# A down stage with a lag of six chunks, and weight statistics and residual loads moved, in a fused linear-attention and feed-forward kernel

## Chip, core and metric

The kernel runs on one core of one Trainium2 chip. The metric is the device time of one execution in microseconds (us). The engines are called by the profile's names: PE (TensorE matmul) and PEld (its weight load), DVE (VectorE), ACT (ScalarE), POOL (GpSimd) and SP (the queue that issues most DMAs). Each of them works through its own instructions in order.

## What is computed

All inputs are bf16. There are 2048 tokens, D = 1024, 32 heads of 32, F = 3584.

```python
xn = layernorm(x)
q, k, v = split(xn @ wqkv)                       # phi(t) = where(t > 0, t + 1, exp(t)) + 1e-6
kv = einsum("bhsd,bhse->bhde", phi(k), v);  z = sum_s phi(k)
s  = (phi(q) @ kv / (phi(q) . z + 1e-6)) @ wo
g  = silu((silu(xn @ w_gate) * (xn @ w_up)) @ w_down)
out = x + s * g
```

## The kernel before

The work has four stages on PE. **KV** (to about 132 us): layer norm, K and V projections and the sum kv over 16 token tiles. **Q and attention** (to 256 us): four blocks of 512 tokens; the Q product of block b+1 runs beside the division (`emit_ND`, L613) of block b, a DMA transpose on SP turns its result (`emit_OT`, L642), and `emit_S` (L647) multiplies by wo. The result s goes to a scratch tensor `s_dram` in DRAM. **Gate and up** (GU) and **down**, both twice: each pass takes 1024 tokens, the upper half first (256 to 430 and 517 to 686 us for GU, 430 to 517 and 686 to 772 us for down).

GU and down use a Strassen-Winograd scheme: every 2x2 block product is made of seven products and not eight. It needs sums of blocks of the activations (S1 to S4) and of the weights (T1 to T4), kept in fp16. The T of the weights are made on chip once, on POOL (`emit_T`, L267, four tensor-tensor operations), and the tile with its T is written to DRAM for the second pass (L286, L287, L290). So that fp16 does not overflow, each weight tile is scaled by a power of two first. That is the **statistics**: a Square with accumulation on ACT (`emit_st0`, L248), a one-column matmul that adds up the partitions (`emit_st1`, L252), and on DVE three small operations and the scaling of the tile (`emit_st2`, L257 to L265).

A weight tile is named by a key: 14 column groups of w_gate ("g") and of w_up ("u"), 14 row groups of w_down ("w"). `prep_q` (L295) lists the keys that are prepared already in the KV and attention stages: 12 of g, 9 of w, and the first g and u last. `prep(n)` makes n steps of this pipeline; a step loads one tile, starts the Square of the previous one and finishes the one before that. Steps are placed by hand: ten in KV (L558), three in the Q product of block 0 (L583), two in the attention of block 0, which stands beside the Q product of block 1, and four in each later block (L674). The other tiles ("raw") are prepared inside GU of the first pass: `pipe`, `pipe1`, `pipe2` for gate and up, `wd_pipe`, `wd_pipe1`, `wd_pipe2` for w_down, one w tile in four iterations.

GU runs over 28 keys, i = 0 to 27. An iteration issues `emit_a(i+1)` (four products of four 128x512 matmuls, banks y, x and the double bank zw), then `emit_b(i)` (three products into x and zw of key i), then `emit_evac(i)`, which on DVE and ACT forms the hidden activations h. Of the zw banks there are two, so the zw products of `emit_a(i+2)` wait for the DVE operation L787 of key i. When all statistics are known, `emit_lam` (L802, eight small DVE operations) derives a factor for each of the 14 row groups, and `scale_h` (L817) multiplies h by it, on ACT or DVE. `emit_hs` (L827) then makes S1 to S4 of a pair of chunks of h for one half of the tokens, four operations on DVE (on POOL for the first pair).

The down stage (`emit_down`, L875) takes 256 tokens at a time as a pair of token tiles t0, t1. A chunk is one of the 14 row groups of w_down. Phase a has four matmuls a chunk (`step_a`), phase b three (`step_b`). The tile t1 follows t0 by `LEAD` = 4 chunks:

```python
NS = NFG + LEAD
for st in range(NS):
    ...
    if st < NFG:
        step_a(t0, st)
        if st == NFG - 1:
            evac_a(t0, hf == 0)
    if st >= LEAD:
        step_a(t1, st - LEAD)
```

PSUM has four single banks (x, y) and two double banks (zw), so with t0 and t1 in flight it is full, and each new tile waits until DVE has emptied the bank of the tile two before. `more_S` and `next_S` are calls of `emit_hs` (with `scale_h` in the first pass) written between the steps. The final pair of the last pass (`finish`, L967) runs t1 eight chunks behind t0 (`LEADZ`), interleaved up to the end of t0, and then the last eight chunks product by product. `fin` (L865) multiplies by s, adds x and writes out; its three engine arguments say who multiplies, adds and issues the store. In `finish` some of these go to POOL (`G`). The residual pieces of x and s that `fin` needs are loaded by `io_load` (L854); five are loaded ahead, at the start of the first GU, and each `fin` loads one more.

DVE, ACT, PE and POOL follow the order of the program; SP too in the attention stage, while in GU and down the order on SP is chosen by the framework's scheduler.

Of the kernel before, what the change touches and what calls it, by code (L numbers as in the profile page):

```python
# [21 lines left out]
def kernel(  # L22
# [39 lines left out]
    NPREP = 12  # L62
    NWE = 9
    LEAD = 4
    LEADZ = 8
# [8 lines left out]
    persist = ctx.enter_context(tc.tile_pool(name="persist", bufs=1))  # L74
    dram = ctx.enter_context(tc.tile_pool(name="dram", bufs=1, space=DRAM))
    xnp = ctx.enter_context(tc.tile_pool(name="xnp", bufs=NB))
    wgu = ctx.enter_context(tc.tile_pool(name="wgu", bufs=NPK))
    stp = ctx.enter_context(tc.tile_pool(name="stp", bufs=4))
    p12 = ExitStack()
    psA = p12.enter_context(tc.tile_pool(name="psA", bufs=3, space=PSUM))  # L80
    ps1 = ExitStack()
    psB = ps1.enter_context(tc.tile_pool(name="psB", bufs=3, space=PSUM))
    psC = ps1.enter_context(tc.tile_pool(name="psC", bufs=2, space=PSUM))
# [33 lines left out]
    w12 = p12.enter_context(tc.tile_pool(name="w12", bufs=1))  # L117
    wo_sb = w12.tile([P, G, D], BF16, name="wo_sb")
    wq_sb = w12.tile([P, DC, D], BF16, name="wq_sb")
    late = p12.enter_context(tc.tile_pool(name="late", bufs=1))  # L120
# [38 lines left out]
    blk12 = blk12_es.enter_context(tc.tile_pool(name="blk12", bufs=2, side="right"))  # L159
    phiw = p12.enter_context(tc.tile_pool(name="phiw", bufs=2))  # L160
# [94 lines left out]
    def emit_st2(key, t, act=False):  # L255
        tot = stp.tile([P, 1], I32, name="tot", tag="tot")
        nc.vector.tensor_scalar(out=tot[:], in0=st_tiles.pop(key).bitcast(I32), scalar1=1, scalar2=0x3f800000,  # L257
                                op0=ALU.logical_shift_right, op1=ALU.bitwise_and)
        c = kcol(key)
        ri, ci = rc_all[:, c:c + 1].bitcast(I32), cs_all[:, c:c + 1].bitcast(I32)  # L260
        nc.vector.tensor_scalar(out=ri, in0=tot[:], scalar1=52 << 23, scalar2=None, op0=ALU.add)
        nc.vector.tensor_scalar(out=ci, in0=ri, scalar1=-1, scalar2=254 << 23, op0=ALU.mult, op1=ALU.add)
        w = raw_view(key, t)
        if not act:
            nc.vector.tensor_scalar(out=w, in0=w, scalar1=cs_all[:, c:c + 1], scalar2=None, op0=ALU.mult)  # L265
# [29 lines left out]
    prep_q = deque(gkeys[2:2 + 2 * NPREP:2] + wkeys[0:NWE] + gkeys[0:2])  # L295
# [33 lines left out]
    with ExitStack() as p1:  # L329
        wpool = p1.enter_context(tc.tile_pool(name="p1w", bufs=1))  # L330
        work = p1.enter_context(tc.tile_pool(name="p1work", bufs=2))
        xnw = p1.enter_context(tc.tile_pool(name="p1xn", bufs=4))
        small = p1.enter_context(tc.tile_pool(name="p1small", bufs=6))
# [214 lines left out]
        for i in range(2, NT):  # L548
            for c in range(NCH):
                emit_Bmm(i, c)  # L550
                if c == 0:
                    if i + 1 < NPE:
                        emit_TR(i + 1)
                    emit_C(i - 1)
                emit_Bev(i, c)
                if i >= 8 and c % 2 == 1:
                    k = 2 * (i - 8) + c // 2
                    prep(2 * (k + 1) // 3 - 2 * k // 3)  # L558
                if c % 2 == 1:
                    for k in (PRE_AT[i - 1] if i - 1 in PRE_AT else (4,) if i == 2 else ())[c // 2:c // 2 + 1]:  # L560
                        emit_N(k)
                    for k in PRE_AT.get(i, ())[c // 2:c // 2 + 1]:
                        ln_pre(k)
            if 3 <= i < 7:
                wt, wv = (wq_sb, wqkv_v) if i < 5 else (wo_sb, wo_v)
                c = (i - 3) % 2
                nc.sync.dma_start(out=wt[:, :, c * CW:(c + 1) * CW], in_=wv[:, :, c * CW:(c + 1) * CW])
# [35 lines left out]
    with ExitStack() as p2:  # L603
        otp = p2.enter_context(tc.tile_pool(name="p2oT", bufs=2))
        work = p2.enter_context(tc.tile_pool(name="p2work", bufs=4))
        small = p2.enter_context(tc.tile_pool(name="p2small", bufs=6))
        blk_es = ExitStack()
        blk = blk_es.enter_context(tc.tile_pool(name="p2blk", bufs=2))
# [60 lines left out]
        def nd_item(b, t):  # L669
            def f():  # L670
                emit_ND(b, t)
                emit_OT(b, t)
                if b > 0 or t % 2 == 1:
                    prep(1)  # L674
            return f
# [23 lines left out]
        sp = ctx.enter_context(tc.tile_pool(name="p3S", bufs=1, side="right"))  # L699
# [7 lines left out]
    with ExitStack() as p3:  # L707
# [10 lines left out]
        def prod(out, lhs, rhs, first):  # L718
            for k in range(HK):
                nc.tensor.matmul(out, lhsT=lhs(k), rhs=rhs(k), start=(first and k == 0), stop=(k == HK - 1),  # L720
                                 skip_group_check=True)
# [42 lines left out]
        def emit_b(key):  # L764
            w = w_tiles[key][:, 0]
            T1, T2, T3, T4 = t_view(w_tiles[key])
            S1, S2, S3, S4, a22 = s_sums[key[0]]
            x1 = xn_blk_tiles[2 * key[0]]
            x_, zw = grp[key][0:2]
            prod(x_[:], lambda k: w[:, HK + k, 0:P], lambda k: x1[:, HK + k, :], False)  # L770
            prod(zw[:, 0, :], lambda k: T4[:, k, :], lambda k: a22[:, k, :], False)
            prod(zw[:, 1, :], lambda k: w[:, HK + k, P:2 * P], lambda k: S4[:, k, :], False)

# [80 lines left out]
        def io_load():  # L854
            if not fq:
                return
            p, t, cc = key = fq.pop(0)
            r0 = p * TB2 + t * P
            pool, tg = (sp, "S%d" % len(fq)) if len(fq) < 3 else (iop, "io")
            io = pool.tile([P, 2, CW], BF16, name="io", tag=tg)  # L860
            nc.sync.dma_start(out=io[:, 0, :], in_=x2[r0:r0 + P, cc * CW:(cc + 1) * CW])
            nc.sync.dma_start(out=io[:, 1, :], in_=s_dram[r0:r0 + P, cc * CW:(cc + 1) * CW])
            io_tiles[key] = io
# [11 lines left out]
        def emit_down(p, h, base, last, more_S, next_S):  # L875
# [91 lines left out]
            def finish(t0, fins):  # L967
                t = t0 + 1
                ks = range(NFG - LEADZ, NFG)
                V, G, S_ = nc.vector, nc.gpsimd, nc.sync  # L970
                for q in (1, 2, 0):
                    for k in ks:
                        prods_b(t, k, True)[q]()
                fins[0]((V, V, S_))
                fins[1]((G, G, nc.gpsimd))
                fins[2]((V, V, S_))
                x_, _, zw = bk[t]
                s1, s34 = kept[t]
                d = m4.tile([P, 2, CW], FP32, name="dd", tag="m4")
                c11 = k2([P, CW], FP32, "c11")[:]  # L980
                hs_ = [slice(i * CW // 2, (i + 1) * CW // 2) for i in range(2)]
                nc.vector.tensor_tensor(out=d[:], in0=zw[:], in1=s34, op=ALU.add)
                for q in range(2):
                    nc.scalar.activation(out=d[:, q, :], in_=d[:, q, :], func=ACT.Silu, scale=rch)
                for cs in hs_:
                    nc.vector.tensor_tensor(out=c11[:, cs], in0=x_[:, cs], in1=s1[:, cs], op=ALU.add)
                    nc.scalar.activation(out=c11[:, cs], in_=c11[:, cs], func=ACT.Silu, scale=rch)
                fin(p, t + TPB, 0, d[:, 0, :], G, G, nc.gpsimd)
                fin(p, t, 1, d[:, 1, :], V, V, S_)
                for cs in hs_:  # L990
                    fin(p, t, 0, c11, V, V, S_, cols=cs)

            NS = NFG + LEAD
            for hf in range(2):
                t0, t1 = 2 * hf, 2 * hf + 1
                for st in range(NS):
                    if hf == 0:
                        if st % 2 == 0 and 3 <= st // 2 + 2 < NWA:
                            more_S(st // 2 + 2)
                        if st >= 12 and st % 2 == 0:  # L1000
# [17 lines left out]
            for hf in (1, 0):  # L1018
# [3 lines left out]
                ld = LEADZ if endz else LEAD  # L1022
                for st in range(NFG + (0 if endz else ld)):
# [4 lines left out]
                    if st >= ld:  # L1028
                        step_b(t1, st - ld, fresh)
                        if fresh and (st - ld) % 2 == 1:  # L1030
                            load_w_to(base + 2 * NWA + (st - ld) // 2 + 2)
                if endz:
                    finish(t0, fins)
# [11 lines left out]
        for pi, p in enumerate(passes):  # L1045
# [6 lines left out]
            if first:  # L1052
                for _ in range(5):
                    io_load()
# [9 lines left out]
            def pipe1(k):  # L1064
                if raw(k):
                    emit_st1(keys[k], grp[keys[k - 2]][4][:, 0:1])

            def pipe2(j):
                if raw(j):
                    emit_st2(keys[j], w_tiles[keys[j]])  # L1070
                    emit_T(keys[j], w_tiles[keys[j]])
# [4 lines left out]
            def wd_pipe(i):  # L1076
                m, r = divmod(i, 4)
# [9 lines left out]
            def wd_pipe1(i):  # L1087
                m, r = divmod(i, 4)
# [3 lines left out]
            def wd_pipe2(i):  # L1092
                m, r = divmod(i, 4)
# [6 lines left out]
                elif r == 3 and m in wd_live:  # L1100
                    emit_st2(*wd_live[m], act=True)

            def more_S(m):
                if first:
                    scale_h(h, 2 * m, nc.scalar)
# [10 lines left out]
            load_w_to(base + na0)  # L1116
            emit_a(keys[0])
            emit_c22(keys[0])
            first_gate[0] = None
            for i in range(n):  # L1120
                load_w_to(base + i + (na0 if i < 24 else min(8, na0 + i - 23)))
# [3 lines left out]
                for j in (range(5) if i == 0 else (i + 4,)):  # L1125
                    pipe(j)
                if first:
                    wd_pipe(i)
                    for k in {25: (0, 2), 26: (4, 5)}.get(i, ()):
                        scale_h(h, k, nc.scalar)  # L1130
                emit_b(keys[i])
                pipe1(i + 3)
# [7 lines left out]
                pipe2(i + 3)  # L1140
                if first:
                    wd_pipe2(i)
                    if i == 24:
                        emit_lam()
                        scale_h(h, 1, nc.vector)
                    elif i == 25:
# [38 lines left out]
```

## Time and profile before

| what | us |
|---|---|
| median of 13 runs | 791.16 (784.94 to 800.64) |
| the profiled execution | 787.8 |
| its span, first to last instruction | 785.9 |
| PE busy / DVE / ACT / POOL | 753.8 / 564.2 / 341.9 / 332.4 |
| last matmul ends, from the span's start | 771.9 |
| last DVE operation ends | 780.0 |
| mean PE clock granted | 0.988 |

A row of a wait list reads: engine, tile and line, who ended the wait, then total us, number of times and the longest. A row of a timeline reads: start in us, duration in us, engine, line, operation, output <- inputs, count. PE is counted busy by the modelled end of a matmul (about 0.38 us each), while in a dense stretch they start 0.216 us apart (eight in 1.73 us), so a hole of PE is read best from the wait list and from the starts.

### The profile page before, as it was taken

How to read it: one execution, taken by the hardware profiler on the slowest of the kernel's cores; microseconds unless marked ns; L12 is line 12 of the kernel's file. 1: busy time of each engine (PE TensorE's matmuls, PEld its weight loads, DVE VectorE, ACT ScalarE, POOL GpSimd, SP SyncE). 2: the span in 40 equal slices, each digit the busy share in tenths (PEclk: the TensorE clock that was granted, in tenths of full speed). 3: DMA queues.
4: the chain of work that ended last, by engine and by line, in shares of the span. 5: the costliest groups of instructions: out<-in, count | busy, mean ns of one | idle time of the engine just before them, and what ended most of it. 6: DMA issues, size and time to landing. Idle time of an engine off the chain costs nothing.

```text
span 785.9 us, 10423 instructions
## 1 busy us (share of the span) xinstructions
PE 753.8 (96%) x3648; PEld 350.0 (45%) x3717; DVE 564.2 (72%) x1034; ACT 341.9 (43%) x472; POOL 332.4 (42%) x451
## 2 busy tenths in 40 slices
PE   7999999999999999999998999999999999999992
PEld 3544444444544444444443444444444444444441
DVE  6788466996776678878888785568767677768256
ACT  2544465897962565566647311132232223201111
POOL 0477179859687237756586033441000000203203
PEclk9999999999999999999999999999999999999997
DMA  9468956489899867878889138289555455503721
GB/s 311 130 155 192 225 207 230 191 237 290 265 320 338 284 249 233 289 261 292 262 284 353 41 105 263 79 321 379 221 182 190 161 167 180 194 36 107 255 87 48
DMA packets 104677, 169.25 MB, mean 215 GB/s; under 512 B 34672, under 2 KB 81392, under 8 KB 94128
## 3 DMA queue, kind: packets, MB, share of 16 engines
q1 hardware_dynamic: 93952, 119.16, 49.3%
q0 software_dynamic: 8224, 45.09, 15.0%
q10 hardware_dynamic: 2448, 4.33, 1.6%
q8 instruction: 29, 0.48, 0.2%
q14 instruction: 24, 0.20, 0.1%
HBM read 110.62 MB, written 50.59 MB: 205 GB/s over the span
## 4 chain that ended last, share of the span: by engine, by line
PE 79%; DVE 10%; DMA 4%; POOL 3%; issue 2%; ACT 1%; SPq 0%; DVEq 0%; POOLq 0%; ACTq 0%
PE zw L720 24%; PE kv_ps L480 14%; PE xb L720 12%; PE dzw L897 10%; PE yb L720 6%; PE dx L897 5%; PE dy L897 3%; PE q_ps L171 2%; DVE o_blk L636 2%; PE s_ps L655 2%; DMA oT<-o_blk 1%; DMA xp<-in_A_x_dram 1%; PE kvz L502 1%; DMA wd<-w_sb 1%; DMA w_sb<-in_B_w_down_dram 1%
## 5 line engine op out<-in xcount | busy, mean ns | idle before, releaser
L720 PEld LDWEIGHTS <-w_sb 128*128 128x128 f16 (+1 forms) x1568 | 152.3, 98 | 187.7 <-issue 5.6
L720 PE MATMUL xb<-xnT,w_sb 128*128 128x512 bf16 x420 | 114.2, 381 | 2.2 <-DVE tot L257 0.6
L480 PE MATMUL kv_ps<-wkv_sb,xnT 128*128 128x512 bf16 x499 | 114.6, 383 | 1.6 <-DMA wkv_sb<-in_A_wqkv_dram 0.7
L720 PE MATMUL zw<-S,w_sb 128*128 128x512 f16 x448 | 106.4, 381 | 2.3 <-POOL hs L838 2.3
L720 PE MATMUL zw<-xnT,w_sb 128*128 128x512 bf16 x448 | 106.1, 380 | 0.0
L277 POOL TENSOR_TENSOR w_sb<-w_sb 128x512 f16<-128x512 bf16 x42 | 48.6, 1158 | 100.3 <-DVE w_sb L265 43.7
L248 ACT ACTIVATE w_sb<-w_sb 128x2048 bf16<-128x2048 bf16 x42 | 79.9, 1902 | 4.3 <-DMA w_sb<-in_B_w_down_dram 3.0
L897 PE MATMUL dx<-w_sb,hT 128*128 128x512 bf16 x216 | 80.7, 379 | 0.3
L480 PEld LDWEIGHTS <-xnT 128*128 128x128 bf16 x512 | 49.1, 98 | 58.1 <-issue 3.1
L897 PEld LDWEIGHTS <-hT 128*128 128x128 bf16 (+1 forms) x448 | 43.8, 98 | 52.9
L897 PE MATMUL dzw<-w_sb,hT 128*128 128x512 bf16 (+1 forms) x217 | 63.8, 379 | 0.0
L655 PE MATMUL s_ps<-wo_sb,oT 128*128 128x512 bf16 x250 | 57.7, 379 | 2.3 <-DMA oT<-o_blk 1.8
L747 DVE SCALAR_TENSOR_TENSOR s<-yb,rc_all,s 128x512 f32<-128x512 f32 x42 | 31.4, 749 | 37.3 <-ACT s L746 37.2
L838 POOL TENSOR_TENSOR hs<-hT 128x512 f16<-128x512 bf16 x2 | 2.3, 1156 | 131.5 <-ACT sg L794 131.4
L171 PE MATMUL q_ps<-xnT,wq_sb 128*128 128x512 bf16 x249 | 57.5, 379 | 0.3
L720 PE MATMUL yb<-S,w_sb 128*128 128x512 f16 x224 | 57.4, 379 | 0.2
L787 DVE SCALAR_TENSOR_TENSOR cg<-zw,rc_all,s 128x1024 f32<-128x1024 f32 x28 | 35.9, 1284 | 27.8 <-PE zw L720 15.1
L794 ACT ACTIVATE sg<-cg 128x1024 bf16<-128x1024 f32 x28 | 29.6, 1057 | 57.2 <-DVE cg L787 57.2
L278 POOL TENSOR_TENSOR w_sb<-w_sb 128x512 f16<-128x512 bf16 x42 | 50.1, 1194 | 3.3
L279 POOL TENSOR_TENSOR w_sb<-w_sb 128x512 f16<-128x512 bf16 x42 | 50.7, 1208 | 0.0
L280 POOL TENSOR_TENSOR w_sb<-w_sb 128x512 f16<-128x512 bf16 x42 | 50.4, 1199 | 0.0
L746 ACT ACTIVATE s<-xb,rc_all 128x512 f32<-128x512 f32 x42 | 28.4, 676 | 39.6 <-issue 35.6
(157 smaller groups left out, 1132.4 us busy)
## 6 DMA issues: line engine op xcount, KB each, us to landing
w_sb<-pk_g SPq DMA_DIRECT2D x26, 1024.0 KB, 6.3
pk_g<-w_sb POOLq DMA_DIRECT2D x14, 1024.0 KB, 4.7
pk_u<-w_sb POOLq DMA_DIRECT2D x14, 1024.0 KB, 5.6
w_sb<-wd SPq DMA_DIRECT2D x14, 1024.0 KB, 5.0
w_sb<-pk_u SPq DMA_DIRECT2D x14, 1024.0 KB, 4.9
w_sb<-wd SPq DMA_DIRECT2D x14, 768.0 KB, 5.7
w_sb<-in_B_w_gate_dram SPq DMA_DIRECT2D x14, 512.0 KB, 7.2
w_sb<-in_B_w_down_dram SPq DMA_DIRECT2D x28, 256.0 KB, 5.9
```

The lines of the kernel that those rows point to most:

```text
L171: nc.tensor.matmul(q_ps[:], lhsT=wq_sb[:, dc, g * P:(g + 1) * P], rhs=xn_ap(dc, btok), start=(dc == 0), stop=(dc == DC - 1))
L248: nc.scalar.activation(out=junk, in_=raw_view(key, t), func=ACT.Square, accum_out=asum[:])
L277: nc.gpsimd.tensor_tensor(out=T1, in0=b12, in1=b11, op=ALU.subtract)
L278: nc.gpsimd.tensor_tensor(out=T2, in0=b22, in1=T1, op=ALU.subtract)
L279: nc.gpsimd.tensor_tensor(out=T3, in0=b22, in1=b12, op=ALU.subtract)
L280: nc.gpsimd.tensor_tensor(out=T4, in0=b21, in1=T2, op=ALU.subtract)
L480: mm = nc.tensor.matmul(kv_ps[:], lhsT=xn_ap(dc, tok), rhs=wkv_sb[:, dc, c * CW:(c + 1) * CW], start=(dc == 0), stop=(dc == DC - 1))
L655: mm = nc.tensor.matmul(s_ps[:], lhsT=oT[:, c, ttok], rhs=wo_sb[:, c, cc * CW:(cc + 1) * CW], start=(c == 0), stop=(c == G - 1))
L720: nc.tensor.matmul(out, lhsT=lhs(k), rhs=rhs(k), start=(first and k == 0), stop=(k == HK - 1), skip_group_check=True)
L747: nc.vector.scalar_tensor_tensor(out=s2[:], in0=y_[:], scalar=rc, in1=s1[:], op0=ALU.mult, op1=ALU.add)
L787: nc.vector.scalar_tensor_tensor(out=d12, in0=zw[:], scalar=rc, in1=s2[:, None, :].to_broadcast([P, 2, TB]), op0=ALU.mult, op1=ALU.add)
L897: nc.tensor.matmul(out, lhsT=lhs, rhs=rhs, start=first, stop=lastk, skip_group_check=True)
```

## The change

- Statistics: `NPREP` 13 and `NWE` 8, so 13 g and 8 w tiles are prepared early; the first g and u come before the last two w. KV takes 11 steps, the attention of block 0 none. In GU of the first pass 13 tiles of gate and up are raw (14 before) and six of w (five before); the w pipeline runs one iteration earlier (`i + 1`). The last u tile has its statistics one iteration earlier, its scaling apart from them (`emit_sc`); `emit_lam` moves from i = 24 to i = 23, and the `scale_h` calls are spread differently.
- Down stage: `LEAD` 6 in place of 4; the more_S and next_S calls are placed accordingly. `LEADZ` is gone: the final pair runs t0 alone, then t1 alone, product by product (both halves of zw over all 14 chunks, then x), with the halves of zw finished before the x product is issued. All of `finish` uses `fin_e`, which in the last pass is DVE, DVE, SP.
- Residuals: the first five `io_load` calls move from the start of GU to the iterations 6 to 10, each made to wait for a matmul of `emit_b(i)`.
- All tile pools get `reuse_waits="tile"` (waits for reused memory tile by tile and not for a whole pool).

```diff
-    NPREP = 12
-    NWE = 9
-    LEAD = 4
-    LEADZ = 8
+    NPREP = 13
+    NWE = 8
+    LEAD = 6
...
-    def emit_st2(key, t, act=False):
+    def emit_st2(key, t, later=False):
...
+        if not later:
+            emit_sc(key, t)
+
+    def emit_sc(key, t):
+        c = kcol(key)
         w = raw_view(key, t)
-        if not act:
-            nc.vector.tensor_scalar(out=w, in0=w, scalar1=cs_all[:, c:c + 1], scalar2=None, op0=ALU.mult)
+        nc.vector.tensor_scalar(out=w, in0=w, scalar1=cs_all[:, c:c + 1], scalar2=None, op0=ALU.mult)
...
-    prep_q = deque(gkeys[2:2 + 2 * NPREP:2] + wkeys[0:NWE] + gkeys[0:2])
+    prep_q = deque(gkeys[2:2 + 2 * NPREP:2] + wkeys[0:NWE - 2] + gkeys[0:2] + wkeys[NWE - 2:NWE])
...
-                    prep(2 * (k + 1) // 3 - 2 * k // 3)
+                    prep(11 * (k + 1) // 16 - 11 * k // 16)
...
-                if b > 0 or t % 2 == 1:
+                if b > 0:
                     prep(1)
...
-        def io_load():
+        def io_load(after=None):
...
-            nc.sync.dma_start(out=io[:, 0, :], in_=x2[r0:r0 + P, cc * CW:(cc + 1) * CW])
-            nc.sync.dma_start(out=io[:, 1, :], in_=s_dram[r0:r0 + P, cc * CW:(cc + 1) * CW])
+            gate([nc.sync.dma_start(out=io[:, 0, :], in_=x2[r0:r0 + P, cc * CW:(cc + 1) * CW]),
+                  nc.sync.dma_start(out=io[:, 1, :], in_=s_dram[r0:r0 + P, cc * CW:(cc + 1) * CW])],
+                 after, sync=True)
...
-            def finish(t0, fins):
...
+            def finish(t):
+                alloc(t, "b")
                 x_, _, zw = bk[t]
                 s1, s34 = kept[t]
+                for q in (1, 2):
+                    for k in range(NFG):
+                        prods_b(t, k, True)[q]()
                 d = m4.tile([P, 2, CW], FP32, name="dd", tag="m4")
                 c11 = k2([P, CW], FP32, "c11")[:]
-                hs_ = [slice(i * CW // 2, (i + 1) * CW // 2) for i in range(2)]
                 nc.vector.tensor_tensor(out=d[:], in0=zw[:], in1=s34, op=ALU.add)
                 for q in range(2):
                     nc.scalar.activation(out=d[:, q, :], in_=d[:, q, :], func=ACT.Silu, scale=rch)
+                fin(p, t + TPB, 0, d[:, 0, :], *fin_e)
+                fin(p, t, 1, d[:, 1, :], *fin_e)
+                for k in range(NFG):
+                    prods_b(t, k, True)[0]()
+                hs_ = [slice(i * CW // 2, (i + 1) * CW // 2) for i in range(2)]
                 for cs in hs_:
                     nc.vector.tensor_tensor(out=c11[:, cs], in0=x_[:, cs], in1=s1[:, cs], op=ALU.add)
                     nc.scalar.activation(out=c11[:, cs], in_=c11[:, cs], func=ACT.Silu, scale=rch)
-                fin(p, t + TPB, 0, d[:, 0, :], G, G, nc.gpsimd)
-                fin(p, t, 1, d[:, 1, :], V, V, S_)
                 for cs in hs_:
-                    fin(p, t, 0, c11, V, V, S_, cols=cs)
+                    fin(p, t, 0, c11, *fin_e, cols=cs)
...
                     if hf == 0:
-                        if st % 2 == 0 and 3 <= st // 2 + 2 < NWA:
-                            more_S(st // 2 + 2)
-                        if st >= 12 and st % 2 == 0:
+                        for m in {2: (3,), 4: (4,), 8: (5, 6)}.get(st, ()):
+                            more_S(m)
+                        if st in (12, 14, 16):
                             next_S((st - 12) // 2)
...
-                m, r = divmod(i, 4)
+                m, r = divmod(i + 1, 4)
...
-                    scale_h(h, 2 * m, nc.scalar)
+                    if m > 3:
+                        scale_h(h, 2 * m, nc.scalar)
                     scale_h(h, 2 * m + 1, nc.vector)
...
+            if first:
+                wd_pipe2(-1)
...
-                    for k in {25: (0, 2), 26: (4, 5)}.get(i, ()):
+                    for k in {n - 4: (0,), n - 3: (2, 4), n - 2: (5, 6)}.get(i, ()):
                         scale_h(h, k, nc.scalar)
-                emit_b(keys[i])
-                pipe1(i + 3)
+                mb = emit_b(keys[i])
+                if first and i in range(6, 11):
+                    io_load(mb)
+                pipe1(i + (4 if i == n - 5 else 3), i)
...
-                pipe2(i + 3)
+                if i == n - 6:
+                    pipe(n - 1)
+                pipe2(i + (4 if i == n - 5 else 3))
                 if first:
                     wd_pipe2(i)
-                    if i == 24:
+                    if i == n - 5:
                         emit_lam()
+                    elif i == n - 4:
+                        emit_sc(keys[-1], w_tiles[keys[-1]])
+                        emit_T(keys[-1], w_tiles[keys[-1]])
                         scale_h(h, 1, nc.vector)
-                    elif i == 25:
+                    elif i == n - 3:
                         scale_h(h, 3, nc.vector)
```

`mb`, the matmul that a gated load waits for, is the last one of the x product, the first of the three products of `emit_b(i)`.

## The prediction

> **What bounds the kernel now.** I read page part 1 first: PE is busy 753.8 of 785.9 us, and no matmul is removed or added, apart from the same 42 statistics columns. So the change can win only what PE idles: the holes between matmuls and the stretch after the last one. The wait list of PE over the whole span (rows of the start-up left out):
>
> ```profile
> PE dzw L897 <- DVE c L941: 2.5, 2, 1.2
> ...
> PE zw L720 <- POOL hs L838: 2.3, 1, 2.3
> PE s_ps L655 <- DMA oT<-o_blk: 1.8, 1, 1.8
> ...
> PE st_ps L252 <- DVE rden L633: 1.1, 2, 0.6
> ...
> PE xb L720 <- DVE tot L257: 0.6, 1, 0.6
> ...
> PE st_ps L252 <- DVE tot L257: 0.4, 1, 0.4
> ```
>
> They sum to 8.7 us of idle. By matmul starts they cost more: the two rows of L897 cost 1.4 us each (1.62 between two starts in place of 0.216). The second row names POOL, but the zw product reads no hs. It waits for two semaphores, and the other is DVE's: the L787 that empties its bank ended at 421.87, hs at 421.92, the matmul started at 421.93. The timeline of DVE shows why L787 was late:
>
> ```profile
> 413.34 1.06 DVE L265 TENSOR_SCALAR w_sb<-w_sb,cs_all 128x2048 bf16<-128x2048 bf16 x1
> ...
> 415.31 0.65 DVE L813 TENSOR_SCALAR lam<-rc_all,hsc 128x14 f32<-128x14 f32 x1
> ...
> 416.07 1.65 DVE L822 TENSOR_SCALAR hT<-hT,lam 128x2048 bf16<-128x2048 bf16 x1
> ...
> 420.60 1.27 DVE L787 SCALAR_TENSOR_TENSOR cu<-zw,rc_all,s 128x1024 bf16<-128x1024 f32 x1
> ```
>
> In one iteration DVE has statistics, a weight scaling, the lambda chain and a scaling of h, without a gap. Last, the timeline of the end, by engine, and the list of L1180 (the program's wrap-up):
>
> ```profile
> 770.02 1.89 PE L897 MATMUL dx<-w_sb,hT 128*128 128x512 bf16 x8
> ...
> 770.80 1.63 DVE L869 TENSOR_TENSOR c<-c,io 128x512 f32<-128x512 f32 x1
> ...
> 776.87 1.52 DVE L870 TENSOR_TENSOR io<-dd,io 128x512 bf16<-128x512 f32 x1
> 778.14 0.58 POOL L871 DMA_DIRECT2D out_dram<-io  x1 [0.30 <-POOL io L870]
> ...
> 779.56 0.42 DVE L870 TENSOR_TENSOR io<-c,io 128x256 bf16<-128x256 f32 x1
> ```
> ```profile
> L1180 POOLq DRAIN  x3: 45/93/7049, 778.1 to 785.7; - x3
> ```
>
> From the last matmul to the end of the span it is 14.0 us. The last store lands at 781.6, but POOL's drain takes 7.05 us, from 778.1 to 785.2, and everybody waits for it.
>
> **Part 1, statistics out of the attention of block 0.** Two steps go, each with a statistics matmul that found its bank held by the division: two waits of 0.55 (L633). The 0.4 us one belongs to block 1 and stays. The steps reappear as one more in KV, where PE runs without holes from 17 to 132 us, and a real last step at the end of block 3. That step puts 0.45 + 0.84 us on DVE ahead of the sums L597 to L600 (240.9 to 249.0), first used at 255.7: still 5 us early. Bounds 0 (the divisions' own lag shows instead) and 1.5; I take **1.1**. The exchange of one g tile for one w tile inside GU takes 1.3 us of DVE work out and puts 2.0 us of ACT work (L1081) in, beside PE; zero, and if ACT had no room (it is busy 12 of 20 us there) 1 us. The pools' finer waits meet no row of the wait list: zero, at best the 0.45 us hole at 132.
>
> **Part 2, residual loads behind attention.** SP's timeline has five loads (L861, 3.98 us of issue, 0.64 MB) between the last two DMA transposes. The last transpose, issued at 243.1, landed at 252.2 (9.1 us; the one before took 5.9) and PE waited 1.8. Moving the loads takes their traffic away: 0.64 MB at about 290 GB/s (mean of that stretch) is 2.2 us. But a w tile's two stores (1.8 MB) now stand where the store of g's tile (1.0 MB) was, at 242. Bounds 0 and 1.8; I take the middle, **0.9**.
> The moved loads put five waits for PE on SP; queued behind each are the next weight loads. The matmul waited for ends about 4.3 us into its iteration (four products of `emit_a` at 0.86, one of `emit_b`). The next g load is issued anyway only at the iteration's end, when a tile comes free: 290.33, 302.44, 314.58 and 326.69, each 0.2 us after the last product. So the gate opens before that; zero. Without this cover a u tile would be late: the one loaded at 311.2 landed at 317.83 and its Square began at 317.94. Upper end 1.5 us for that and the extra traffic.
>
> **Part 3, the statistics' end in GU.** The hole at 421.9 costs 2.47 us, and afterwards the starts are 0.43 us apart for 3.4 us, half clock: 1.7 more. [...] by the row 4.2. The trace decides (a 2.37 us hole at 12.4 was followed by half clock too; 1.8 at 252 was not): 4.2 is at stake.
> After the change, iteration 24 loses the statistics (0.5) and the lambda chain (1.85) on DVE. Iteration 23 gains 1.85 and loses a scaling (0.8): +1.05. There DVE had 0.26 us to spare before L787 (its idle before 411.58), which then ends at 413.6 where PE wants it by 413.4: a hole of about 0.25. In iteration 24 DVE is later by 0.8 and earlier by 2.4, so L787 ends about 420.3 where PE wants 419.7: 0.55. Together 0.8, too short for the clock to fall. **4.2 - 0.8 = 3.4**; bounds 4.2, and 1.7 if the holes add up to about 2.5 but not in one piece.
>
> **Part 4, lag of six.** The two 1.4 us holes arise because t1 of the next half comes four chunks (3.5 us) after t0, while DVE still empties banks behind two `next_S`. In the trace DVE finishes that work (L941 at 460.79) 10.4 us after t0 of the first half ended. With seven t1 steps of 0.864 left (6.05) and six solo steps of the next t0 (5.2), that bank is wanted at 12.5: both holes go, **2.8**. What is late next is S3 for chunk 6. Its pair m = 3 is needed after six solo steps, 5.2 us after the stage begins, where it was 6.9. The DVE timeline around the first pass's start at 430.5:
>
> ```profile
> 435.23 0.75 DVE L822 TENSOR_SCALAR hT<-hT,lam 128x2048 bf16<-128x2048 bf16 x1
> 436.08 0.42 DVE L838 TENSOR_TENSOR S<-hT 128x512 f16<-128x512 bf16 x1
> 436.54 0.42 DVE L839 TENSOR_TENSOR S<-S,hT 128x512 f16<-128x512 f16 x1
> 436.88 0.42 DVE L840 TENSOR_TENSOR S<-hT 128x512 f16<-128x512 bf16 x1
> ```
>
> DVE has no gap before them and the calls stay in their order, so S2 is there at 436.96 and PE wants it at 435.9, S3 at 437.3 against 436.1: a new hole of 1.2. In the second pass (stage from 685.7, no scaling) S2 comes at 691.33 against 691.14, S3 at 691.66 against 691.35: 0.3. Later pairs fit. Net **1.3**; bounds 2.8, and -0.5 if DVE's clearing shifts with the lag.
>
> **Part 5, the tail.** PE's matmuls are the same, t1's last product is now x alone: 14 x 0.216 = 3.0 us. Let E be the end of the pair before (753.9 in the trace). DVE then runs, in order: the six `fin` of that pair until E+9.6 (763.5 in the trace); t0's sum, 1.23; wait for the silu, 1.2 more; three `fin` at 1.33, to E+16.05; t1's zw sum to 17.3; silu 0.7; two `fin` to 20.75; then for x two half sums (0.4), a silu (0.45) and two half `fin`, to E+23.15. The last matmul is at E+18.3, so DVE ends 4.85 after it, against 8.1 now: 3.2 us gained, because without POOL beside it a `fin` costs 1.33 (755.0 to 763.5: six in 8.5 with one gap) and not up to 3.2. The stores on SP take 0.35 us of issue each and SP is idle otherwise. After the last store (1.65 to land) the wrap-up is 0.3 + 0.75 when nobody drains late: the drain after 778.1 moves to POOL's last work, near 745, and is over long before the end. That is 3.2 more, 785.9 against 782.7.
> [...] by the row of 7049 ns it saves 6.4. I take the row, less 0.2 for DVE's order: **6.2**. Bounds 7.0 and 4.5.
>
> **The sum.** 1.1 + 0.9 + 3.4 + 1.3 + 6.2 = 12.9. The span goes from 785.9 to 773.0, that execution from 787.8 to 774.9. The median of the runs shown is 3.4 above that execution; with the same distance the new median is 791.16 - 12.9 = 778.3.
>
> **Rivals.**
> *A, DVE only hands its lateness on.* In parts 3 and 4 DVE is the late engine and keeps almost all its work. Part 4 brings nothing and part 3 only 1.7: 1.1 + 0.9 + 1.7 + 6.2 = 9.9, 781.3. For it: DVE runs without a gap from 428 to 445 and in iterations 23 to 25. Against it: the arithmetic above, which counts that work.
> *B, every hole goes.* 1.5 + 1.8 + 4.2 + 2.8 + 7.0 = 17.3, 773.9. It needs DVE about 1 us earlier at both stage starts; nothing in the diff gives that.
> *C, the end is not relieved.* POOL's drain takes long whenever it comes, or waits for all; then the tail saves 0 to 3.2 and the time is about 783. Against it: the drain began when POOL's own last work began, not when the others ended.
> *D, slower: the gates starve GU.* If SP reaches a gate before the u load that belongs in front of it, that load comes an iteration late (6.05 us), of which the cover in GU takes up to about 1. Its Square blocks ACT, then PE, and a hole over 2.3 brings 1.7 of half clock. At most 5.1 for each of five gates, 25.5 in all: 791.2 - 12.9 + 25.5 = 803.8. It decides from 3.4 us a gate on. For it: the slack of 0.1 us at 317.8, and SP's order in GU is not written by hand. Against it: the gate opens before the tile that the next load needs.
> *E, it does not do what it says.* New holes at GU's first iterations or in KV eat most of it: 789.
>
> **Chances.** Forecast 0.62, A 0.18, B 0.08, C 0.06, E 0.04, D 0.02. A difference under 0.5% (4.0 us) is about what a measurement of this kernel cannot tell from none. Faster by more 0.94, within 0.5% 0.04, slower 0.02. The range takes in A, B and C, the bounds of the parts, and a median's own scatter: 772 to 785.
>
> **What would show it.** After: no drain row of POOL near the end, last store about 0.3 us before the wrap-up; no L869 or L870 on POOL in the last 20 us; the clock 1.0 around 420; the L897 wait for L941 gone and a wait of about 1.2 us for hs or S (L839, L840) six chunks into the first down stage; last DVE operation about 5 us after the last matmul. I am wrong if PE waits in GU iterations 6 to 12, if the half clock stays, or if a DVE operation other than S delays the down stage.

## The result, and the profile after

The changed kernel takes 778.89 us (median of 11 runs); the kernel before, beside it, 791.12 (median of 48). The ratio of the two is 0.9864, 95% interval 0.9836 to 0.9892, so it is faster by 10.8 us (8.5 to 13.0). The ratio leaves out slow executions, those over 1.5% above the fastest of their kernel, so it is not the quotient of the two medians. The forecast was 778.3. The profiled execution takes 778.17 us, its span 776.4, 9.5 less than before, at a granted clock of 0.994. The sum behind the forecast was 12.9.

Where the 9.5 us come from is read best by cutting each span at five matmuls that every kernel has. The stretches below are times between them on the profiled core: to the last `kvz` matmul (key/value stage), to the first `s_ps` (mostly attention of block 0), to the first `xb` (the rest of attention and the projection), to the first `dx` (gate/up with the statistics in it), to the end of the last matmul (down stage), and to the end of the span (tail). The last column tells where the granted clock fell to half before the tail. The first stretch lies between 128.9 and 132.4 us in the fourteen profiles told of here, and the three with half clock at 11 to 13 us are the three longest, so a difference there says nothing of the edits.

| kernel | key/value | block 0 | to gate/up | gate/up | down | tail | span | half clock at |
|---|---|---|---|---|---|---|---|---|
| before | 132.36 | 37.98 | 86.19 | 173.98 | 341.39 | 14.03 | 785.9 | 13, 423 |
| after | 132.30 | 36.41 | 86.27 | 173.28 | 340.22 | 7.91 | 776.4 | 13 |
| gain | 0.06 | 1.57 | -0.08 | 0.70 | 1.17 | 6.12 | 9.5 | |
| predicted | 0 | parts 1 and 2: 2.0 | | 3.4 | 1.3 | 6.2 | 12.9 | |

The wait list of PE over the span of the changed kernel, some rows left out (us in total, times, longest):

```profile
PE zw L723 <- DVE cg L792: 1.7, 1, 1.7
...
PE st_ps L251 <- ACT w_sb L247: 1.4, 1, 1.4
PE xb L723 <- DVE hT L790: 1.3, 1, 1.3
PE dy L903 <- DVE S L844: 1.0, 1, 1.0
...
PE s_ps L658 <- DMA oT<-o_blk: 0.6, 1, 0.6
...
PE st_ps L251 <- DVE rden L636: 0.3, 1, 0.3
```

Of the rows of before, the 2.5 of dzw for `c` is gone, a zw wait of 1.7 stands near the place of the one of 2.3, the oT row fell from 1.8 to 0.6, and of the rden row's 1.1 us 0.3 is left. Three of the new rows matter below: the statistics matmul waiting for a Square on ScalarE (at 237.8), xb for hT (at 406.2) and dy for S (at 434.8). The zw wait at 415.3 did not bring half clock in this execution. In the tail, GpSimd's drain (the DRAIN row of the program's wrap-up) has moved away: of the three drains on that line (shortest, median, longest in ns, first and last start) the first, which is the long one, now begins at 738.0 and is over by 744.9.

```profile
L1194 POOLq DRAIN  x3: 45/102/6886, 738.0 to 776.1; - x3
```

The last operation of VectorE ends at 773.89, 5.4 us after the last matmul's end (768.48). The last store lands at 775.48 and the wrap-up begins at 775.57.

### The profile page after: what moved, and what is told of

The parts are those of the page before. It is cut to its first block, busy times and chain, and to the rows that moved or that the text cites. A ratio compares the mean times of both kernels' runs of the same rounds, so it can differ in the third digit from the quotient of the medians.

```text
span 776.4 us, 10413 instructions
## 1 busy us (share of the span) xinstructions
PE 752.1 (97%) x3648; PEld 349.2 (45%) x3717; DVE 565.8 (73%) x1037; ACT 345.3 (44%) x473; POOL 325.7 (42%) x445
## 5 line engine op out<-in xcount | busy, mean ns | idle before, releaser
L750 ACT ACTIVATE s<-xb,rcl 128x512 f32<-128x512 f32 x14 | 9.6, 687 | 64.9 <-PE xb L723 64.9
```

## The experiments

All are the changed kernel with one thing altered, unless said otherwise. Each is told by its timed ratio to the kernel before, and by the one stretch that its edit touches. The intervals of the ratios are 4 to 16 us wide, so most verdicts rest on stretches. The down stage repeats within 0.04 us in eight of ten profiles that keep after's lag and order of S (0.44 more in `t_dve` and `sq_lam`). Gate/up lies at 173.17 to 173.35 in five of eight with after's code (174.1 in two, 175.8 in one with half clock), and at 171.22 to 171.29 in all five with the last Square moved. To gate/up scatters by 4 us.

**The earlier finish** (`t_old`): `finish`, its order of the products and LEADZ = 8 put back, so that t1 runs eight chunks behind t0 again (the expectation's words on a reciprocal mean this).

```
-            def finish(t):
+            def finish(t0, fins):
...
+                V, G, S_ = nc.vector, nc.gpsimd, nc.sync
...
+                fins[1]((G, G, nc.gpsimd))
```

> The changed kernel with the earlier finish put back (the reciprocal runs eight columns ahead, the two column series interleaved, GpSimd taking half of the last adds and products). Theory (the tail is worth what the profile of after says, 6.1 us): the time rises by about 6, to 784.5; from the last matmul to the end of the span 14 us in place of 7.95, with a GpSimd drain of about 7 us in it. Rival (most of the 6 us came from other edits near the end, the tail alone is half): +3.

Measured: ratio 0.9957 (0.9933 to 0.998), median 785.27; tail 14.03 us, exactly that of before, and its drain is the old one:

```profile
L1197 POOLq DRAIN  x3: 45/93/7049, 776.8 to 784.4; - x3
```

The theory holds: the tail alone is worth 6.1 us, about two thirds of the 9.5 by which the spans differ.

**The earlier order, without GpSimd** (`t_dve`): as above with `V, G, S_ = nc.vector, nc.vector, nc.sync`, so every `fin` is on VectorE and SyncE.

> The earlier order of the finish, with all its adds and products on VectorE and its stores on SyncE: no GpSimd work near the end. Theory (taking GpSimd out is most of the gain, the product-by-product order the rest): about +1.2, the last matmul to the end of the span 9.1 us in place of 7.95. Rival (order and engine matter alike): +3, 11 us.

Measured: ratio 0.990 (0.9873 to 0.9927); tail 9.55. So taking GpSimd out is worth 14.03 - 9.55 = 4.5 us, and the product-by-product order the other 1.6. (The down stage is 0.44 longer here, by one wait at 544, far from `finish`.)

**One store back on GpSimd's queue** (`drain`), no arithmetic:

```
-                fin(p, t, 1, d[:, 1, :], *fin_e)
+                fin(p, t, 1, d[:, 1, :], nc.vector, nc.vector, nc.gpsimd)
```

> The changed kernel, with one store of the finish issued by GpSimd's queue in place of SyncE's; no arithmetic moves. Theory (GpSimd's drain at the end is long because its queue still has a store of its own, and it lasts about 6.5 us after the issue): a drain row on GpSimd of 6 to 7 us, and the time +2.7. Rival ([...]the long one came with GpSimd's arithmetic): no such row, +0.1.

Measured: ratio 0.992 (0.9883 to 0.9958); tail 10.74, so +2.83. GpSimd had been idle for 32.9 us when it issued that store, and the drain's start is 773.95:

```profile
773.98 0.54 POOL L877 DMA_DIRECT2D out_dram<-io  x1 [32.92 <-DVE io L876]
```
```profile
L1194 POOLq DRAIN  x3: 45/93/6929, 774.0 to 781.4; - x3
```

Everything else had ended when SyncE's own drain began at 778.1; GpSimd's ended at 780.9. A drain of 6.9 to 7.05 us stands behind GpSimd's last instruction in all fourteen profiles, be it the store after its own arithmetic or a lone one. It sets the end in the three profiles in which it begins 3.8 to 4.2 us before the others are done (before, `t_old`, `drain`), and costs nothing in the others, where it begins at 738.5 or earlier.

**The lag of four again** (`lead4`): `LEAD = 6` back to `4`, and the `more_S` and `next_S` steps where they were.

> The changed kernel with the pair lag set back to 4 chunks and the steps between the passes where they were. Theory (the profile's holes say what the lag is worth): the two TensorE holes of 1.4 us (near 461 and 716) come back, those near 435 and 689 (1.6 in all) shrink to about 0.3: +1.2. Rival (the lag only moves the wait): 0.

```profile
PE dzw L903 <- DVE c L947: 2.5, 2, 1.2
```

Measured: the row of before is back, the S row is gone, the down stage takes 341.40 (before 341.39, after 340.22): +1.18. The time, 778.46 with ratio 0.9888 (0.9858 to 0.9919), cannot show it.

**The residual loads ungated** (`io_early`):

```
+                for _ in range(5):
+                    io_load()
                 first_gate[0] = marks[("S", NB - 1, 0)]
...
-                if first and i in range(6, 11):
-                    io_load(mb)
```

> The changed kernel with the five residual loads ungated again, at the place in the queue they had. Theory (their traffic slows the last transposing transfer of the attention output): TensorE's hole near 250 grows from 0.6 to about 1.8 us, the transfer takes longer than 10.2 us: +1.2. Rival (that transfer takes 10 us either way; the hole shrank because it was issued earlier): 0.

Measured: ratio 0.9867 (0.9769 to 0.9965), too wide to use. But the hole it was to open is smaller, 0.44 us. SyncE's timeline shows the five loads issued right ahead of the last transpose:

```profile
236.15 4.42 SPq L866 DMA_DIRECT2D io<-in_A_x_dram  x5
242.46 0.33 SPq L224 DMA_DIRECT2D w_sb<-pk_g  x1
242.89 1.91 SPq L648 DMA_TRANSPOSE oT<-o_blk  x1
```

That transpose landed at 250.53, 7.6 us after its issue. In after it took 10.2 without those loads (issued at 240.43), and in the other runs 7.5 to 11.2. The theory falls: the residual loads do not set it. Something else goes with it. In the three profiles where the last transpose was issued after the one before it had landed (before by 0.06 us, `sq_hs3` by 1.2, `io_early` by 2.1) it took 9.1, 7.5 and 7.6; in the other eleven, issued up to 0.35 us before that landing, 9.7 to 11.2. Whether this is the cause, no run shows. The gate/up stretch is 173.35 with the loads ungated and 173.28 gated, so the gates cost nothing either.

**The statistics' steps where they were** (`prep_b0`): `prep(2 * (k + 1) // 3 - 2 * k // 3)` in the key/value stage, and `if b > 0 or t % 2 == 1` in attention.

> The changed kernel with the statistics' steps where they were before (part of them inside the attention of block 0). Theory (what the profile of after shows: 0.8 us of holes in attention came off, a new one of 1.4 us near 237.8 was put on): between -0.6 and 0. Rival (the step forecast for this edit, 1.1 us gained by it): +1.1.

Measured: the two waits for `rden` return (at 152.4 and 161.4), and block 0 takes 38.04 again (+1.6); ratio 0.9856 (0.9772 to 0.9941).

```profile
PE st_ps L251 <- DVE rden L636: 1.1, 2, 0.6
```

The stretch after it takes 87.12 in this kernel (here the oT wait is 3.0 us) and 86.19 in before. Over the ten profiles here with the new placement and the gates, that stretch lies between 86.27 and 90.68, mean 87.8. So block 0 gains 1.6, and on the mean 1.1 of it is given back (87.8 against the mean 86.7 of those two). Net about 0.4, in a stretch that scatters by 4 us: neither the theory nor the rival is settled.

**The last Square one step later** (`sq_top`). In after, `pipe(n - 1)` puts the Square of the last u tile right ahead of the scale that the next product's sum needs. ScalarE's timeline of after:

```profile
400.46 1.91 ACT L247 ACTIVATE w_sb<-w_sb 128x2048 bf16<-128x2048 bf16 x1 [0.20 <-DMA w_sb<-in_B_w_up_dram]
...
402.37 0.67 ACT L750 ACTIVATE s<-xb,rc_all 128x512 f32<-128x512 f32 x1
```

The Square waited 0.20 us for its load (landed 400.36), and `s` (L750) waited for the Square, though the xb that it reads was complete at 399.63 and ScalarE's operation before was over at 400.26. So of the 2.1 us that `s` was late, 1.9 are the Square's own length and 0.2 its load; the expectation puts too much on the load. VectorE then had nothing to do for 2.17 us:

```profile
403.07 0.75 DVE L751 SCALAR_TENSOR_TENSOR s<-yb,rc_all,s 128x512 f32<-128x512 f32 x1 [2.17 <-ACT s L750]
```

The edit:

```
-                for j in (range(5) if i == 0 else (i + 4,) if i < n - 6 else ()):
+                for j in (range(5) if i == 0 else (i + 4,) if i < n - 6 or i == n - 5 else ()):
...
-                if i == n - 6:
-                    pipe(n - 1)
```

> The changed kernel with the last Square of the u statistics on ScalarE moved one step later, behind the product-critical scale of that step, so that nothing waits behind its load. Theory (the Square waited for its load and pushed ScalarE's next scale, and by it VectorE's hT, late): the holes near 406 and 407 (1.7 us) go and the one near 415 shrinks by up to 1.4: -2.7. Rival (VectorE is late on its own[...]): the holes only move, -0.3.

Measured: ratio 0.9753 (0.9671 to 0.9836). ScalarE now does `s` first:

```profile
397.74 0.67 ACT L750 ACTIVATE s<-xb,rc_all 128x512 f32<-128x512 f32 x1
398.31 1.90 ACT L247 ACTIVATE w_sb<-w_sb 128x2048 bf16<-128x2048 bf16 x1
```

The wait of xb for hT is gone, the zw wait is 1.6 instead of 1.7: the gate/up stretch fell by 2.0, to 171.27. The theory was right about the holes near 406 and wrong that the one near 415 would shrink. The span of its profile is 4.4 below after's; the other 2.4 are the first stretch (2.7 shorter) and the one to gate/up, which the edit does not touch.

**The lambda chain split on top** (`sq_lam`): the first twelve columns made two iterations earlier, the last two, one of them an iteration earlier, by operations with one tensor and per-partition scalars (the new helper for a column is shown).

```
+        def lam_col(k):
+            c = rcl[:, k:k + 1]
+            nc.vector.tensor_scalar(out=c, in0=rc_all[:, 2 * k:2 * k + 1], scalar1=rc_all[:, 2 * k + 1:2 * k + 2],
+                                    scalar2=rcw[:, k:k + 1], op0=ALU.mult, op1=ALU.mult)
```

> As the run before (the last Square one step later), and the lambda chain split: most columns made earlier, the last column by operations with one tensor input, so that no VectorE operation with two tensor inputs stands beside GpSimd's. Theory (the two-input operations of lambda each ended with a GpSimd operation and cost 1.4 us more than alone): the hole near 415 goes, another -1 against the run before. Rival (lambda is not what the PE waits for): 0 against it.

The reason was this pair of views of after. VectorE's lambda products of 128x14, 0.16 and 0.17 us long in before:

```profile
408.67 0.68 DVE L810 TENSOR_TENSOR rcl<-rc_all 128x14 f32<-128x14 f32 x1
409.38 1.07 DVE L811 TENSOR_TENSOR rcl<-rcl,rc_all 128x14 f32<-128x14 f32 x1
```

and GpSimd's differences beside them, which end at 409.32 and 410.43, each within 0.03 us of the end of VectorE's:

```profile
407.43 1.89 POOL L281 TENSOR_TENSOR w_sb<-w_sb 128x512 f16<-128x512 bf16 x1
409.28 1.15 POOL L282 TENSOR_TENSOR w_sb<-w_sb 128x512 f16<-128x512 bf16 x1
```

Measured: ratio 0.9816 (0.9737 to 0.9894). The zw wait fell to 0.5, but a wait for `cu` of 0.8 and a longer one for S (1.2, in `sq_top` 1.0) came behind it; gate/up 171.22 against 171.27, the down stage 0.4 longer by the wait for S. Nothing gained: here VectorE did hand its lateness on. And the cure was only half one: an operation with a single tensor input took 0.98 us too, and ended at 408.23, when GpSimd's had ended at 408.20 (what ties the two ends together, no trace shows):

```profile
407.25 0.98 DVE L827 TENSOR_SCALAR lam<-rc_all,hsc 128x14 f32<-128x14 f32 x1
```
```profile
407.05 1.15 POOL L281 TENSOR_TENSOR w_sb<-w_sb 128x512 f16<-128x512 bf16 x1
```

The operations of one column beside it stayed at 0.15 to 0.27.

**After and sq_top once more, side by side** (`after_again`, `sq_top_again`).

> The changed kernel itself once more, as the measure for the three runs after it. Every run with its attention stage so far showed a wait for a statistics Square near 237 of 1.4 to 2.9 us (one of them at 208 too); theory (the loads of the statistics are late in every execution): again 1.4 us or more, stretch from the end of the key/value stage to the first gate product 123 to 127 us. Rival (that was chance): under 0.5 us. The time itself 778 to 780.

> The last Square of the u statistics one step later, timed beside the changed kernel. Theory (that Square's wait for its load is what held the end of the gate/up stage): 2.0 us under the run before by the profile of the first try (stretch from the first gate product to the first down product 171.3 in place of 173.3 to 174.1), so -2 to -3. Rival (the first try's 773.8 was a lucky set): 0 to -0.5.

Measured: 776.58, ratio 0.9876 (0.9828 to 0.9925), and 779.34, ratio 0.9899 (0.9843 to 0.9954). The profiles repeat their stretches: gate/up 173.28 and 171.27. The timed runs do not resolve those 2.0 us: they spread from 775.8 to 784.5 and from 774.0 to 785.5, the longer ones at a lower clock (0.997 and 0.991 at the ends of the first). The wait for the Square near 235 was 1.5 and 2.3 us. It was there, in one place or another, in all eleven profiles with the statistics' steps as in after. In `lead4` the row names `rden`, which ended at 237.06, but the Square, kept 3.17 us by its load, had ended only at 237.02, so without `rden` the wait would have been as long.

**S earlier** (`sq_hs3`, on top of sq_top): the S of the chunk pair m = 3 is made in the last iteration of gate/up, right behind that of pair 2, and not two steps into the down stage. (The expectation calls it the third product.)

```
-                        for m in {2: (3,), 4: (4,), 8: (5, 6)}.get(st, ()):
+                        for m in {4: (4,), 8: (5, 6)}.get(st, ()):
...
             def tail():
                 emit_hs(h, 0, 2, nc.vector)
+                more_S(3)
```

> As the run before, and the third product of the next pass's statistics issued ahead of the tail's lambda work, so that S is there earlier. Theory (the holes near 431 and 685, 1.24 and 0.36 us, are the wait for S): both go to about 0.2 or less, the stretch of the down stage 338.7 in place of 340.0: -1.3. Rival (VectorE hands its lateness on, as the split lambda chain did): the hole comes back at another product, 0.

Measured: 777.23, ratio 0.9855 (0.9811 to 0.9899). No row for S is left in the wait list (by starts 0.4 us of the 1.6 remains), and the down stage takes 338.97 against 340.23: -1.26. The theory holds; the stretch says so, the time cannot.

**Twelve statistics steps in the key/value stage** (`sq_hs3_kv12`, on top): `prep(12 * (k + 1) // 16 - 12 * k // 16)`.

> As the run before, with 12 in place of 11 statistics steps in the key/value stage, so that the last one falls a step earlier in the attention of block 1. Theory (the wait near 237 is that of the last step alone, whose load has only just been issued): it goes, -1.4 to -2. Rival (the loads of all steps there come late, since each waits for GpSimd to hand back a slot): the wait stays at another step, 0.

Measured: 775.55, ratio 0.9839 (0.9796 to 0.9882), span 770.4. The wait for the Square is gone, but an o_blk wait of 1.0 (block 0: 37.19, +0.76) and an oT wait of 1.9 stand in its place; block 0 and the stretch after it take 123.2 together against 124.3. It has the shortest profile of all, 4.2 us below that of after in the same set; by time the interval overlaps after's, so "better than after" is shown by the stretches only.

## Why the prediction was right, and where it was not

**Part 5, the tail: right in size, and nearly so in split.** 6.2 predicted, 6.12 measured and undone by `t_old`. Of it 2.66 is VectorE's earlier end (3.0 predicted, with the 0.2 for its order taken off; it ends 5.4 us after the last matmul and not 4.85), and 3.45 is the stretch behind it (3.2 predicted). To count the row of 7049 ns as part of the end was right: `drain` isolates it at 6.9 us. Rival C is refuted.

**Part 4, the lag: right.** 1.3 predicted; in the first pass the wait for S cost 1.24 us by matmul starts, in the second 0.36, the net was 1.17, and `lead4` turned it back by 1.18. S was late in VectorE's order, as argued: with S made earlier in that order (`sq_hs3`) the stage is 1.26 shorter. Rival B, which had no such hole, falls with it.

**Part 3, the statistics' end: the failed step.** "Together 0.8, too short for the clock to fall" was 3.75 by matmul starts: 1.41 at 406, 0.33 at 407, 1.91 at 415 and 0.10 at 404, so the stage gained 0.7 instead of 3.4, below the lower bound of 1.7. The clock did not fall, but in `t_old`, with nearly the same holes, it did. The step counted VectorE's operations and not what the moved step puts on ScalarE: the last Square, 1.9 us long, in front of `s`. That is 2.0 of the 2.7 missing, shown by `sq_top` in two profiles and by the three kernels built on it. The other term was the lambda chain, taken at 1.85 us from before and 3.1 in after (408.67 to 411.77), where GpSimd's differences of the last w tile now stand beside it and two of its products took 0.68 and 1.07 us, not 0.16 and 0.17. That this chain sets the rest is not shown: with it split by `sq_lam` the wait moved on, which is rival A's mechanism, at part 3's end only.

**The half clock.** The prediction read the trace of before so that a hole of 2.3 us brings it and one of 1.8 does not. Over the 14 profiles this does not stand as put. Half clock followed holes of 1.81 us (`t_old`, at 415.7), 2.04, 2.33 and 2.86, and did not follow holes of 1.81 (`t_dve`, the same place), 2.26, 2.63 and 2.98 (`prep_b0`). What best tells them apart is a grid: in each profile all changes of the clock lie a multiple of 3.413 us apart (in before, 120 steps from 13.47 to 423.07). Adding up PE's idle time inside each step of that grid, the clock fell before the tail after seven steps, six with 2.04 us or more and one with 1.97 (`t_old`), and after none with 1.87 or less; one step with 2.01 was spared (`sq_top_again`). The hole of 2.98 lay 1.87 in one step and 1.1 in the next. Two steps of `t_old` and two of `t_dve` (a row: window and its length, busy us of PE, PEld, DVE, ACT and POOL with counts, granted clock, DMA share, GB/s):

```profile
412.71:416.12 3.41, 1.44 (x6) 0.57 (x6) 3.27 (x5) 2.80 (x4) 0.00 (x0) 1.00 1.00 308
416.12:419.54 3.42, 3.42 (x10) 1.20 (x9) 2.21 (x4) 3.42 (x4) 3.06 (x3) 0.50 0.51 204
```
```profile
413.36:416.77 3.41, 1.60 (x8) 0.68 (x7) 3.24 (x4) 2.80 (x5) 0.75 (x1) 1.00 0.97 352
416.77:420.18 3.41, 3.41 (x18) 1.57 (x16) 3.06 (x5) 3.41 (x3) 3.33 (x4) 1.00 0.45 129
```

PE was idle for 1.97 us of the first step above and for 1.81 of the third. So counting the 1.7 us of half clock was right for the hole of 2.3 in before, where one step held 2.27 of it, and partly luck: where the grid falls was not known. After's 1.75 at 415 is below the 1.87 after which no profile shows a fall. In `t_old` it was 1.81 with 0.16 more idle time in the same step, and gate/up took 1.7 longer than in `t_dve`.

**Parts 1 and 2: near by luck, the reasons half wrong.** 2.0 predicted, 1.57 - 0.08 = 1.49 measured. But after's stretch to gate/up is the shortest of the ten above; by their mean the pair is worth about 0.4. Block 0's part was 1.6, just above its upper bound of 1.5: by starts each of the two waits cost 0.72 and not 0.55 (0.777 from the `nd_ps` matmul before, in place of 0.06), and 0.12 came off the third. As for the step put at the end of block 3, "still 5 us early" looked at the sums and not at the step's own load. ScalarE waited 3.09 us for it:

```profile
235.74 1.91 ACT L247 ACTIVATE w_sb<-w_sb 128x2048 bf16<-128x2048 bf16 x1 [3.09 <-DMA w_sb<-in_B_w_down_dram]
```

That load was issued only at 228.9, behind a transpose on SyncE, and PE waited 1.4. It was offset by the oT wait, 1.8 to 0.6, which I ascribed to the residual loads' traffic; the transpose took 10.2 us instead of 9.1, so it was not faster, only issued 2.6 us earlier (240.43 against 243.07; 1.6 of that is block 0's gain), and `io_early`, one profile, speaks against the traffic. Rival D is refuted: in gate/up the gates cost 0.1 us or less, and PE waits for nothing between 265.2 and 403 in after. The pools' finer waits were put at nothing or 0.45 at 132; the hole there went from 0.44 to 0.42, and no run takes `reuse_waits` back alone.

**The total.** Against the spans of these two executions the sum was 3.4 too high, 2.7 of it in part 3. Rival A's sum of 9.9 is nearer to 9.5, though it had nothing from part 4 and more from part 3 than came. The forecast in us still met the median because of the step from the profile to the median: I carried over the 3.4 us by which before's median lay above its profile, while after's lies only 0.7 above its own. That is luck, not a proof of the 12.9.

## What to carry to other kernels

When a step is moved, list what it issues on every engine, and for each such instruction what it must wait for there: a Square on an engine with slack still stalls the chain if the chain's own operation is queued behind it (by its length of 1.9 us at the end of gate/up), or if its load has only just been issued (by a wait of 3.1 us at the end of attention). Count a queue's drain as part of the end if that queue has work in the last few microseconds (GpSimd's, 6.9 us behind one store in `drain`, made the tail 2.8 us longer). And where a change is worth 1 to 2 us in executions that scatter by 8, judge it by stretches between fixed instructions of the profile, not by the span.

## What the hardware showed that was not expected

GpSimd's drain lasts 6.9 to 7.05 us, after arithmetic with stores or after a lone store's issue, beside 4.1 us on PE, at most 1.5 on ScalarE and 0.5 on VectorE. The falls of the clock went with PE's idle time in one step of a 3.413 us grid (1.97 us or more in the seven steps that one followed, and 2.01 in one that none followed), not with the length of a hole (one of 1.81 us was followed by half clock, one of 2.98 was not). Most VectorE products of 14 columns took between 0.43 and 1.08 us while GpSimd subtracted, and ended within 0.05 us of one of its operations; in before two took 0.16 and 0.17 where it computed nothing, and one 0.17 beside it (at 415.99), as did one in `sq_top` (at 405.00). The reduction of 14 columns in the same chain stayed at 0.17, one-column operations at 0.14 to 0.27. The last DMA transpose took 7.5 to 11.2 us between issue and landing, the two shortest without the residual loads ahead of it (7.5) and with them (7.6).
